# Earlier weight sums, paired snapshots and scaling moved to the output stage, in a linear-attention plus bilinear-FFN kernel

## The chip, the cores and the metric

The kernel runs on one core of a Trainium2 chip, as one program in one launch. The metric is device time in microseconds (us), from the start of the program to its end; lower is better. Engines are named as in the profile: PE is TensorE (PEld its weight loads), DVE is VectorE, ACT is ScalarE, POOL is GpSimd, and SP is the engine whose queue issues nearly all DMA transfers.

## The reference

The input is q, k and v of shape (4, 8, 768, 64) and one decay `lam` per head. A causal linear attention with decay is followed by a bilinear feed-forward network over 3072 tokens:

```python
for b in range(nb):                       # blocks of the sequence
    intra = np.einsum('bhic,bhjc->bhij', qb, kb) * Dmask[None]
    intra = np.einsum('bhij,bhjd->bhid', intra, vb)
    inter = np.einsum('bhid,bhde->bhie', qb * lam_pow[None], kv_state)
    out[:, :, sl] = intra + inter
    kv_state = lam_block * kv_state + np.einsum('bhsd,bhse->bhde', kb_dec, vb)
...
a = x @ w_a          # x: (3072, 512), the attention output; w_a, w_b: (512, 1536)
b = x @ w_b
return (a * b @ w_out).astype(np.float32)   # w_out: (1536, 512)
```

## The kernel before, in words

The tokens are cut into 24 units of 128 (6 units for each of the 4 batches). A unit's attention needs: its q, k and v loaded (`load_x`, three 256 KB transfers issued by SP); q and k scaled by powers of `lam` into one bf16 tile `qk` (`prep_k`: units 4 and 5 have k scaled on DVE and q on POOL, later units have both on POOL); that tile transposed (units 4 to 6 by PE, `piece_T`; from unit 7 on by a transposing DMA that SP issues, `dma_start_transpose`); v cast to bf16 (`prep_v`: POOL up to unit 6, DVE from unit 7); the scores on PE and their mask on DVE (`piece_S`, tiles `kq` and `m`); the state update (`piece_V`, tiles `kvd` and `st`); and the output (`pieces_O`), which ACT writes to the FFN's input `xT`.

The FFN takes the units in groups of 4, 1, 2, 4, 4, 4, 4 and 1 (groups 0 to 7). Groups 0, 1, 2 and 7 are computed directly: for each of 12 slices f of d_ff a product `a_ps`, a copy by ACT, a product `b_ps`, and the elementwise product `ab` by DVE, and after that the output products `op`. Groups 3 to 6 (`ffn_seven`) take pairs of slices (i = 0 to 5) with seven 128 by 256 products instead of eight. For this they need sums of the weights: `w_sums` makes the tile `tw` of pair i out of `wa_sb` and `wb_sb` with four elementwise sums of 128x512 bf16, and `sums` makes four sums `xs` of the group's `xT` on DVE. In `step(i, n)`, n names the product: the accumulating PSUM banks are copied by ACT at points in between (`snap`, tiles `s1`, `s2`, `s5`, `u2`), DVE adds `c12` and `c22`, and POOL adds `c11` out of the snapshots of products 1 and 2 and multiplies `c11` by `c12` into `ab`. The snapshot `s1` has two buffers and `s2` one.

The order of the work is written out by hand in `PLAN`: for each group a list of (slot, letter, unit). A group calls `hook(slot)` after each slice f (slots 0 to 11) and then in its output stage (from slot 12: for groups 3 to 6 two slots for each of the four output tiles, 12 to 19). P is `prep_k` and `prep_v` of a unit (PK and PV one of them), V, S, O, O2 and Q are pieces of the attention, C a weight cast, TW one call of `w_sums`, W the store of a kept output tile. Each engine runs its instructions strictly in the order in which they are issued here, and so does SP's queue.

Loads are issued ahead by `pump`, which is called after each weight cast and each `prep_v`. A unit may be loaded as long as it is less than `LOOKAHEAD` units beyond the last one whose q and k were scaled. A transfer also waits for a free buffer: q and k have three buffers each, v has four. Weights land in the pool `wst` (12 buffers of 4 KB per partition), which afterwards holds `tw`, `xs` and the kept outputs `o_kept` of the first seven units too; the outputs of later units go through three buffers `o_sb`.

Of the kernel before, what the change touches and what calls it, by code (L numbers as in the profile page):

```python
# [16 lines left out]
F32 = mybir.dt.float32  # L17
# [5 lines left out]
def _bc(ap, dims):  # L23
# [8 lines left out]
W_BUFS = 12  # L32
LOOKAHEAD = {9: 2, 10: 1}
# [10 lines left out]
PLAN = {  # L44
# [23 lines left out]


@with_exitstack  # L70
def kernel(
# [11 lines left out]
    nc = tc.nc  # L83
# [47 lines left out]

    def load_x(w, u):
        b, nb = divmod(u, NB)
        t = ld_pool.tile([128, H, D], F32, name=w + "f", tag=w + "f", bufs=4 if w == "v" else 3)
        nc.sync.dma_start(out=t, in_={"q": qr, "k": kr, "v": vr}[w][b, nb])  # L135
        raw[u, w] = t

# [55 lines left out]
    def pump():  # L193
        while pending:
            kind, c = pending[0]
            if kind in "abo":
                if len(staged) >= W_BUFS:
                    return
            elif c >= used["u"] + LOOKAHEAD.get(used["u"], 2 if used["u"] > 8 else 3):
                return  # L200
            pending.pop(0)
            if kind in "abo":
                load_w(kind, c)
            else:
                load_x(kind, c)
# [323 lines left out]
    def ffn_seven(g, u0, xT, hook):  # L529
# [20 lines left out]

        x11, x12, x22 = xT[:, 0:2, 0:256], xT[:, 2:4, 0:256], xT[:, 2:4, 256:512]

        def snap(name, ps, bufs):
            t = sn_pool.tile([128, 2, 256], F32, name=name, tag=name, bufs=bufs)
            nc.scalar.copy(t, ps)  # L555
            return t

        def step(i, n):
            d = live.setdefault(i, {})
            if n == 1:  # L560
                d["q"], d["qb"] = bank_of("m_q")
                product(i, d["q"], w_of(wa_sb, 0, i), x11, True)
                d["s1"] = snap("s1", d["q"], 2)
            elif n == 5:
                d["r"], d["rb"] = bank_of("m_r")
                product(i, d["r"], t_of(0, i), st[:, 0], True)
# [1 line left out]
            elif n == 2:  # L568
                p, pb = bank_of("m_p")
                product(i, p, w_of(wa_sb, 2, i), x12, True)  # L570
                s2 = snap("s2", p, 1)
                bank["held"].discard(pb)
                d["c11"] = a_pool.tile([128, 2, 256], BF16, name="c11", tag="a")
                nc.gpsimd.tensor_add(d["c11"], d["s1"], s2)  # L574
# [325 lines left out]
```

## Time and profile before

| | |
|---|---|
| median of 3 runs | 246.71 us (245.89 to 247.68) |
| the profiled execution | 246.64 us, of which the span from first to last instruction is 244.6 us |
| PE busy | 219.7 us, 90% |
| DVE, ACT, POOL busy | 145.1, 112.5 and 126.1 us |
| mean granted PE clock | 0.985 of full speed |

In answers on lines and waits, "out<-in" are the program's tile names, and what stands in brackets behind an instruction is the time that its engine sat idle before it and what ended this idle time. Times are from the start of the span.

### The profile page before, as it was taken

The page shows a single profiled execution, that of the slowest core. Times are in us where ns is not written, and L with a number is a line of the kernel's source. Part 1 is how long each engine was busy: PE and PEld are TensorE (multiplying, and loading weights), DVE is VectorE, ACT ScalarE, POOL GpSimd, SP SyncE. Part 2 cuts the span into 40 slices and gives each one's busy share as a digit, 9 for nine tenths or more (in the row PEclk, how much of TensorE's full clock was granted, in tenths as well). Part 3 has the DMA queues.
Part 4 walks back from the last instruction along what each step waited for, and adds up shares of the span by engine and source line. Part 5 has one row for each costly group of instructions (what it writes and reads, how often), then busy time and mean ns, then how long its engine had stood idle before and what let it go on. Part 6 is the DMA issues. An engine that isn't in the chain of part 4 may idle for free.

```text
span 244.6 us, 5389 instructions
## 1 busy us (share of the span) xinstructions
PE 219.7 (90%) x2108; PEld 151.2 (62%) x2127; DVE 145.1 (59%) x253; ACT 112.5 (46%) x220; POOL 126.1 (52%) x129
## 2 busy tenths in 40 slices
PE   7789999977996878499899979999979999999994
PEld 2565444446685646378555868546868547885493
DVE  1984748352679947647947746917757634664050
ACT  3685570153542136267124757235655236773151
POOL 6060001599995146968800899800999303874000
PEclk9999999997999999979999999999999999999999
DMA  4999999996819999990899398894590212000211
GB/s 146 302 288 350 374 386 288 231 214 132 133 36 179 184 190 221 227 216 4 170 163 387 113 197 137 170 176 171 24 193 14 50 71 86 0 3 6 102 68 44
DMA packets 97545, 39.41 MB, mean 161 GB/s; under 512 B 85488, under 2 KB 92016, under 8 KB 97520
## 3 DMA queue, kind: packets, MB, share of 16 engines
q1 hardware_dynamic: 97232, 39.00, 70.6%
q8 instruction: 16, 0.26, 0.5%
q10 hardware_dynamic: 288, 0.07, 0.1%
q14 instruction: 9, 0.07, 0.1%
HBM read 28.32 MB, written 6.29 MB: 141 GB/s over the span
## 4 chain that ended last, share of the span: by engine, by line
PE 56%; DMA 17%; POOL 8%; issue 6%; SPq 5%; DVE 5%; ACT 2%; POOLq 0%; DVEq 0%; ACTq 0%
PE op L642 18%; PE m_q L541 14%; PE m_r L541 7%; DMA qf<-in_q_dram 4%; PE a_ps L474 4%; PE b_ps L474 4%; DMA wst<-in_moe_w_a_dram 3%; PE m_p L541 3%; DMA wst<-in_moe_w_b_dram 3%; SPq L135 3%; POOL qk L281 3%; DMA kf<-in_k_dram 2%; PE o_ps L371 2%; DMA q<-in_q_dram 2%; DMA vf<-in_v_dram 2%
## 5 line engine op out<-in xcount | busy, mean ns | idle before, releaser
L642 PE MATMUL op<-wo_sb,ab 128*128 128x512 bf16 (+2 forms) x295 | 64.2, 362 | 1.5 <-issue 0.8
L574 POOL TENSOR_TENSOR c<-s,s 128x512 bf16<-128x512 f32 x24 | 30.5, 1272 | 44.9 <-ACT s L555 44.8
L541 PEld LDWEIGHTS <-tw 128*128 128x128 bf16 x384 | 37.8, 99 | 14.9 <-issue 7.2
L642 PEld LDWEIGHTS <-ab 128*128 128x128 bf16 x312 | 28.0, 98 | 27.8
L501 DVE TENSOR_TENSOR ab<-a_sb,b_ps 128x128 bf16<-128x128 bf16 (+2 forms) x48 | 19.3, 417 | 29.4 <-ACT a_sb L483 21.7
L281 POOL TENSOR_TENSOR qk<-qf,lp_q 128x512 bf16<-128x512 f32 x20 | 22.1, 1107 | 21.8 <-DMA qf<-in_q_dram 21.8
L354 DVE TENSOR_TENSOR m<-kq,lotri 128x512 bf16<-128x512 f32 x47 | 29.5, 684 | 5.2 <-PE kq L337 4.9
L541 PE MATMUL m_q<-xs,tw 128*128 128x256 bf16 x192 | 29.2, 275 | 2.7 <-ACT u L555 2.7
L583 POOL TENSOR_TENSOR ab<-c,c 128x512 bf16<-128x512 bf16 x24 | 28.2, 1174 | 4.4 <-DVE c L581 3.8
L474 PE MATMUL a_ps<-xT,wa_sb 128*128 128x128 bf16 (+2 forms) x198 | 28.3, 272 | 2.3 <-DVE ab L501 1.4
L474 PE MATMUL b_ps<-xT,wb_sb 128*128 128x128 bf16 (+2 forms) x192 | 28.1, 276 | 0.1
L590 DVE TENSOR_TENSOR ab<-c,m_q 128x512 bf16<-128x512 f32 x24 | 16.5, 687 | 19.3 <-PE m_q L541 19.3
L483 ACT CAST a_sb<-a_ps 128x128 bf16<-128x128 f32 (+2 forms) x48 | 17.4, 376 | 18.3 <-PE a_ps L474 15.4
L281 POOL TENSOR_TENSOR qk<-kf,lp_k 128x512 bf16<-128x512 f32 x18 | 19.1, 1063 | 11.3 <-DMA kf<-in_k_dram 8.7
L394 ACT CAST xT<-o_ps 128x512 bf16<-128x512 f32 (+1 forms) x24 | 12.2, 556 | 26.6 <-PE o_ps L371 26.5
L637 ACT COPY o_sb<-op 128x512 f32<-128x512 f32 (+2 forms) x19 | 10.3, 542 | 30.0 <-PE op L642 30.0
L474 PEld LDWEIGHTS <-wa_sb 128*128 128x128 bf16 x200 | 16.7, 101 | 9.3 <-issue 1.5
L581 DVE TENSOR_TENSOR c<-u,m_r 128x512 f32<-128x512 f32 x24 | 16.4, 682 | 8.7 <-ACT u L555 8.4
L541 PEld LDWEIGHTS <-wa_sb 128*128 128x128 bf16 x192 | 18.8, 99 | 3.0
L474 PEld LDWEIGHTS <-wb_sb 128*128 128x128 bf16 x192 | 16.1, 100 | 6.0 <-ACT wb_sb L174 0.2
L555 ACT COPY s<-m_r 128x512 f32<-128x512 f32 x24 | 14.1, 588 | 10.8 <-PE m_r L541 10.8
L555 ACT COPY s<-m_q 128x512 f32<-128x512 f32 x24 | 14.2, 590 | 10.6 <-PE m_q L541 10.2
(88 smaller groups left out, 307.5 us busy)
## 6 DMA issues: line engine op xcount, KB each, us to landing
vf<-in_v_dram SPq DMA_DIRECT2D x24, 256.0 KB, 4.9
qf<-in_q_dram SPq DMA_DIRECT2D x20, 256.0 KB, 4.2
kf<-in_k_dram SPq DMA_DIRECT2D x20, 256.0 KB, 4.6
out_dram<-o_sb SPq DMA_DIRECT2D x16, 256.0 KB, 2.1
wst<-in_moe_w_a_dram SPq DMA_DIRECT2D x6, 512.0 KB, 8.4
wst<-in_moe_w_b_dram SPq DMA_DIRECT2D x6, 512.0 KB, 8.8
wst<-in_moe_w_out_dram SPq DMA_DIRECT2D x6, 512.0 KB, 10.5
out_dram<-o_kept SPq DMA_DIRECT2D x7, 256.0 KB, 4.1
```

The costliest lines, as they stand in the source:

```text
L281: eng_of(eng).tensor_mul(dst.rearrange("p (c b) d -> p b c d", b=2), x[:].rearrange("p (b c) d -> p b c d", b=2), lp.rearrange("p (b c) o ...
L354: nc.vector.tensor_mul(m, kq[i], lotri_bc)
L474: nc.tensor.matmul(ps[:, lo:hi], lhsT=w_sb[:, s, f * 128:(f + 1) * 128], rhs=xT[:, s, lo:hi], start=(s == 0), stop=(s == KS - 1), skip_gro ...
L483: nc.scalar.copy(a_sb[:, :gt], ps[:, :gt])
L501: nc.vector.tensor_mul(ab[:, f, :gt], a_sb[:, :gt], ps[:, :gt])
L541: nc.tensor.matmul(ps[:, f, :], lhsT=w(k, f), rhs=x[:, k, :], start=(first and f == 0 and k == 0), stop=True, skip_group_check=True)
L555: nc.scalar.copy(t, ps)
L574: nc.gpsimd.tensor_add(d["c11"], d["s1"], s2)
L581: nc.vector.tensor_add(c12, d["u2"], d["r"])
L583: nc.gpsimd.tensor_mul(ab[:, 2 * i:2 * i + 2, 0:256], d["c11"], c12)
L590: nc.vector.tensor_mul(ab[:, 2 * i:2 * i + 2, 256:512], d["c22"], d["q"])
L642: nc.tensor.matmul(op[:, lo:hi], lhsT=ab[:, f, t * 128:(t + 1) * 128], rhs=wo_sb[:, f, lo:hi], start=(f == 0), stop=(f == FC - 1))
```

## The change

The edits, in the order of the diff:

- In groups 3, 4 and 5 the scaling and casting of units (P) leaves the product stage (slots 1, 3 and 9) for the output stage (slots 12, 14, 16, 18). Group 3 keeps two at slots 1 and 3 (units 13 and 14). The pieces Q, V and O2 of the output stage move one slot later.
- The six `w_sums` move: pairs 0 and 1 stay on POOL but are issued at slots 13 and 16 of group 0; pairs 2 and 3 go to DVE at slots 30 and 32 of group 0; pairs 4 and 5 stay on DVE, at slot 4 of group 1 and slot 15 of group 2.
- The pool `wst` has two more buffers (14), and v has three buffers instead of four.
- `pump` may load three units ahead instead of two from unit 17 on.
- The snapshots `s1` and `s2` become the halves of one tile `s12` out of the pool `wst`.

```diff
 for _g, _u in ((3, 11), (4, 15), (5, 19)):
     PLAN.setdefault(_g, []).extend(
-        [(1, "P", _u + 2), (3, "P", _u + 3), (9, "P", _u + 4), (11, "V", _u),
-         (12, "Q", (_u, _u + 1, _u + 2, _u + 3)), (14, "V", _u + 2),
-         (16, "O2", (_u + 2, _u + 3)), (18, "S", _u + 4)])
+        [(11, "V", _u), (12, "P", _u + 4), (13, "Q", (_u, _u + 1, _u + 2, _u + 3)),
+         (15, "V", _u + 2), (17, "O2", (_u + 2, _u + 3)), (18, "S", _u + 4)])
     if _u + 5 < 24:
-        PLAN[_g] += [(12, "P", _u + 5), (19, "S", _u + 5)]
+        PLAN[_g] += [(14, "P", _u + 5), (16, "P", _u + 6), (18, "P", _u + 7), (19, "S", _u + 5)]
+PLAN[3] += [(1, "P", 13), (3, "P", 14)]
 PLAN[3] += [(_s, "W", None) for _s in range(12, 19)]
-PLAN[0] += [(_s, "TW", (_f, "pool")) for _s, _f in ((31, 0), (34, 1))]
-PLAN[1] += [(_s, "TW", (_f, "pool")) for _s, _f in ((8, 2), (11, 3))]
-PLAN[2] += [(_s, "TW", (_f, "dve")) for _s, _f in ((3, 4), (5, 5))]
+PLAN[0] += [(_s, "TW", _f) for _s, _f in ((13, (0, "pool")), (16, (1, "pool")), (30, (2, "dve")),
+                                          (32, (3, "dve")))]
+PLAN[1] += [(4, "TW", (4, "dve"))]
+PLAN[2] += [(15, "TW", (5, "dve"))]
...
-    wst_pool = ctx.enter_context(tc.tile_pool(name="wst", bufs=W_BUFS))
+    wst_pool = ctx.enter_context(tc.tile_pool(name="wst", bufs=W_BUFS + 2))
...
-        t = ld_pool.tile([128, H, D], F32, name=w + "f", tag=w + "f", bufs=4 if w == "v" else 3)
+        t = ld_pool.tile([128, H, D], F32, name=w + "f", tag=w + "f", bufs=3)
...
-            elif c >= used["u"] + LOOKAHEAD.get(used["u"], 2 if used["u"] > 8 else 3):
+            elif c >= used["u"] + LOOKAHEAD.get(used["u"], 2 if 8 < used["u"] < 17 else 3):
...
-                d["s1"] = snap("s1", d["q"], 2)
+                d["s12"] = wst_pool.tile([128, 2, 2, 256], F32, name="s12", tag="wst")
+                snap("s1", d["q"], 0, d["s12"][:, 0])
...
-                s2 = snap("s2", p, 1)
+                snap("s2", p, 0, d["s12"][:, 1])
...
-                nc.gpsimd.tensor_add(d["c11"], d["s1"], s2)
+                nc.gpsimd.tensor_add(d["c11"], d["s12"][:, 0], d["s12"][:, 1])
```

How this moves instructions shows at three places (the number behind a tile's name tells one buffer's use from another). The first is POOL, from the last cast of weights in the front of the program to the work on unit 5. Before, q of unit 4 (`qk_690`) comes first, and the eight sums of pairs 0 and 1 (`tw_744`, `tw_780`) stand between it and q of unit 5 (`qk_788`):

```order
L178 CAST wa_sb_96<-wst_126 128x4x128
L281 TENSOR_TENSOR qk_690<-qf_495,lp_q_165 128x2x4x64
L300 CAST vb_740<-vf_534 128x512
L509 TENSOR_TENSOR tw_744<-wb_sb_97,wa_sb_96 128x512
L510 TENSOR_TENSOR tw_744<-wb_sb_97,tw_744 128x512
L511 TENSOR_TENSOR tw_744<-wb_sb_97 128x512
L512 TENSOR_TENSOR tw_744<-wa_sb_96,tw_744 128x512
L509 TENSOR_TENSOR tw_780<-wb_sb_97,wa_sb_96 128x512
L510 TENSOR_TENSOR tw_780<-wb_sb_97,tw_780 128x512
L511 TENSOR_TENSOR tw_780<-wb_sb_97 128x512
L512 TENSOR_TENSOR tw_780<-wa_sb_96,tw_780 128x512
L281 TENSOR_TENSOR qk_788<-qf_536,lp_q_165 128x2x4x64
```

In the change the same eight sums (`tw_668`, `tw_680`) stand ahead of q of unit 4 (`qk_700`) and of unit 5 (`qk_798`):

```order
L179 CAST wa_sb_96<-wst_126 128x4x128
L510 TENSOR_TENSOR tw_668<-wb_sb_97,wa_sb_96 128x512
L511 TENSOR_TENSOR tw_668<-wb_sb_97,tw_668 128x512
L512 TENSOR_TENSOR tw_668<-wb_sb_97 128x512
L513 TENSOR_TENSOR tw_668<-wa_sb_96,tw_668 128x512
L510 TENSOR_TENSOR tw_680<-wb_sb_97,wa_sb_96 128x512
L511 TENSOR_TENSOR tw_680<-wb_sb_97,tw_680 128x512
L512 TENSOR_TENSOR tw_680<-wb_sb_97 128x512
L513 TENSOR_TENSOR tw_680<-wa_sb_96,tw_680 128x512
L282 TENSOR_TENSOR qk_700<-qf_495,lp_q_165 128x2x4x64
L301 CAST vb_750<-vf_534 128x512
L282 TENSOR_TENSOR qk_798<-qf_536,lp_q_165 128x2x4x64
```

What moved: POOL does its eight sums before any unit's data, and q and v of units 4 and 5 then follow each other directly. The sums of pairs 2 and 3, which stood behind the v of unit 6, are gone from POOL.

The second place is DVE, from the second mask of unit 4 (`m1`) into the first products of group 1 (`ab`). Before, k of unit 5 (`qk_788`) follows the mask:

```order
L354 TENSOR_TENSOR m1_736<-kq1_725,lotri_149 128x512
L281 TENSOR_TENSOR qk_788<-kf_538,lp_k_166 128x2x4x64
L501 TENSOR_TENSOR ab_800<-a_sb_806,b_ps_808 128x128
L434 TENSOR_TENSOR st0_156<-kvd_312,bdiag_152 128x512
L501 TENSOR_TENSOR ab_800<-a_sb_824,b_ps_826 128x128
L501 TENSOR_TENSOR ab_800<-a_sb_837,b_ps_839 128x128
```

In the change:

```order
L355 TENSOR_TENSOR m1_746<-kq1_735,lotri_149 128x512
L510 TENSOR_TENSOR tw_752<-wb_sb_97,wa_sb_96 128x512
L511 TENSOR_TENSOR tw_752<-wb_sb_97,tw_752 128x512
L512 TENSOR_TENSOR tw_752<-wb_sb_97 128x512
L513 TENSOR_TENSOR tw_752<-wa_sb_96,tw_752 128x512
L510 TENSOR_TENSOR tw_763<-wb_sb_97,wa_sb_96 128x512
L511 TENSOR_TENSOR tw_763<-wb_sb_97,tw_763 128x512
L512 TENSOR_TENSOR tw_763<-wb_sb_97 128x512
L513 TENSOR_TENSOR tw_763<-wa_sb_96,tw_763 128x512
L282 TENSOR_TENSOR qk_798<-kf_538,lp_k_166 128x2x4x64
L502 TENSOR_TENSOR ab_810<-a_sb_816,b_ps_818 128x128
L435 TENSOR_TENSOR st0_156<-kvd_312,bdiag_152 128x512
```

What moved: the eight sums of pairs 2 and 3 (`tw_752`, `tw_763`) now stand ahead of k of unit 5 (`qk_798`), and with it ahead of everything that DVE does for group 1. A little further on, the four sums of pair 4 (`tw_895`) stand between the fifth and the sixth `ab` of group 1, where nothing stood before:

```order
L502 TENSOR_TENSOR ab_810<-a_sb_871,b_ps_873 128x128
L502 TENSOR_TENSOR ab_810<-a_sb_887,b_ps_889 128x128
L510 TENSOR_TENSOR tw_895<-wb_sb_97,wa_sb_96 128x512
L511 TENSOR_TENSOR tw_895<-wb_sb_97,tw_895 128x512
L512 TENSOR_TENSOR tw_895<-wb_sb_97 128x512
L513 TENSOR_TENSOR tw_895<-wa_sb_96,tw_895 128x512
```

The third place is SP's queue from the transposition of unit 15 on, with which the output stage of group 3 begins. Before, units 15 and 16 (`qkT_1751`, `qkT_1931`) are transposed, and the loads of units 17 and 18 issued, when the first store of the output stage comes:

```order
L309 DMA_TRANSPOSE qkT_1751<-qk_1748 128x8x128
L135 DMA qf_1755<-in_q_dram 128x8x64
L135 DMA kf_1757<-in_k_dram 128x8x64
L135 DMA vf_1759<-in_v_dram 128x8x64
L309 DMA_TRANSPOSE qkT_1931<-qk_1928 128x8x128
L135 DMA qf_1935<-in_q_dram 128x8x64
L135 DMA kf_1937<-in_k_dram 128x8x64
L135 DMA vf_1939<-in_v_dram 128x8x64
L626 DMA out_0_dram<-o_kept_751 128x512
L638 DMA out_0_dram<-o_sb_1948 128x512
L626 DMA out_0_dram<-o_kept_751 128x512
```

In the change the transposition of unit 16 (`qkT_1943`) stands behind three stores, and the loads of two units follow it:

```order
L310 DMA_TRANSPOSE qkT_1850<-qk_1847 128x8x128
L136 DMA qf_1854<-in_q_dram 128x8x64
L136 DMA kf_1856<-in_k_dram 128x8x64
L136 DMA vf_1858<-in_v_dram 128x8x64
L629 DMA out_0_dram<-o_kept_761 128x512
L641 DMA out_0_dram<-o_sb_1867 128x512
L629 DMA out_0_dram<-o_kept_761 128x512
L310 DMA_TRANSPOSE qkT_1943<-qk_1940 128x8x128
L136 DMA qf_1947<-in_q_dram 128x8x64
L136 DMA kf_1949<-in_k_dram 128x8x64
L136 DMA vf_1951<-in_v_dram 128x8x64
L136 DMA qf_1953<-in_q_dram 128x8x64
```

What moved: transpositions and loads of units 16 to 18 now alternate with the stores of the output stage, where before they stood ahead of them or in the next product stage.

More of the change, by code (lines that the diff above doesn't have):

```diff
@@ L551, in ffn_seven, with snap @@
         x11, x12, x22 = xT[:, 0:2, 0:256], xT[:, 2:4, 0:256], xT[:, 2:4, 256:512]
-        def snap(name, ps, bufs):
-            t = sn_pool.tile([128, 2, 256], F32, name=name, tag=name, bufs=bufs)
+        def snap(name, ps, bufs, t=None):
+            if t is None:
+                t = sn_pool.tile([128, 2, 256], F32, name=name, tag=name, bufs=bufs)
             nc.scalar.copy(t, ps)
```

## The prediction

> **What bounds the kernel now.** I read the engines' shares on the page first, then the list of who waited for whom on PE (in total, times, longest, us), then PE's granted clock in 40 slices of the span, and by stage (a row begins with the stretch, its length and PE's busy time; the clock is the number ahead of the DMA share).
>
> ```profile
> PE 219.7 (90%) x2108; PEld 151.2 (62%) x2127; DVE 145.1 (59%) x253; ACT 112.5 (46%) x220; POOL 126.1 (52%) x129
> PE tps L323 <- POOL qk L281: 3.1, 1, 3.1
> PE m_q L541 <- ACT u L555: 2.7, 4, 1.1
> PE m_r L541 <- DVE ab L590: 2.0, 1, 2.0
> PE m_q L541 <- DVE c L587: 1.4, 1, 1.4
> PE a_ps L474 <- DVE ab L501: 1.4, 1, 1.4
> PE kq L337 <- DVE ab L501: 1.4, 2, 0.8
> PE o_ps L371 <- DVE st L434: 1.2, 1, 1.2
> PE m_r L541 <- DVE xs L521: 1.1, 1, 1.1
> PE kq L337 <- DVE ab L590: 0.8, 2, 0.4
> PEclk9999999997999999979999999999999999999999
> 56.80:59.40 2.60, 2.60 (x25) 2.60 (x26) 0.29 (x1) 1.44 (x3) 2.60 (x4) 0.50 0.61 140
> 104.20:106.80 2.60, 2.60 (x14) 1.86 (x13) 0.85 (x2) 1.43 (x3) 2.15 (x2) 0.50 1.23 221
> 133.20:153.50 20.30, 18.88 (x174) 16.35 (x170) 13.09 (x21) 13.30 (x25) 17.78 (x16) 1.00 0.77 161
> 203.20:221.50 18.30, 18.30 (x167) 16.03 (x165) 10.11 (x17) 13.31 (x25) 13.12 (x11) 1.00 0.04 16
> ```
>
> PE is the bound: busy 219.7 of 244.6 us, and beside PE's own weight loads no engine reaches 60%. So time is won only where PE waits or runs at a lower clock. The nine waits add up to 15.1 us. Two slices fall below 9 tenths, behind two long waits: there PE ran 2.6 us at clock 0.50, which lost half of it, 1.3 us each; behind the other waits the clock stayed. The last two rows are the product stages of groups 4 and 6: group 4, with q and k scaled in between, leaves PE idle for 1.4 us; group 6, which has no such work, for nothing. All that can be won here is 15.1 + 2.6 = **17.7 us**. I go through these waits by place, each with what comes late next.
>
> **Unit 5's transposition (waits 3.1, half clock 1.3).**
>
> ```profile
> 25.79 1.05 ACT L174 CAST wb_sb<-wst 128x1024 bf16<-128x1024 f32 x1 [1.64 <-DMA wst<-in_moe_w_b_dram]
> 40.56 1.04 POOL L281 TENSOR_TENSOR qk<-qf,lp_q 128x512 bf16<-128x512 f32 x1 [21.79 <-DMA qf<-in_q_dram]
> 67.90 1.15 POOL L512 TENSOR_TENSOR tw<-wa_sb,tw 128x512 bf16<-128x512 bf16 x1
> 45.53 0.61 POOL L300 CAST vb<-vf 128x512 bf16<-128x512 f32 x1 [3.92 <-DMA vf<-in_v_dram]
> 56.79 1.03 PE L323 MATMUL tps<-ident,qk 128*128 128x128 bf16 x8 [3.12 <-POOL qk L281]
> 49.97 1.30 DVE L281 TENSOR_TENSOR qk<-kf,lp_k 128x512 bf16<-128x512 f32 x1
> 74.80 1.26 DVE L512 TENSOR_TENSOR tw<-wa_sb,tw 128x512 bf16<-128x512 bf16 x1
> 78.11 0.42 DVE L512 TENSOR_TENSOR tw<-wa_sb,tw 128x512 bf16<-128x512 bf16 x1
> 73.38 1.22 POOL L281 TENSOR_TENSOR qk<-kf,lp_k 128x512 bf16<-128x512 f32 x1
> ```
>
> PE reached this transposition at 53.7 and waited for q of unit 5, which stood behind eight sums on POOL. In the change these sums (1.15 us each, 9.2 in all) run in POOL's idle 21.8 us: they need the weights of pairs 0 and 1 and a free buffer, and the buffers that come free first held the weights whose cast ends at 26.8. So they end at about 27 + 9.2 = 36.2, ahead of 40.56: cost nothing. Were they to start after 31, they would push q of unit 4. q of unit 5 then goes as soon as its data are there: v of unit 4 landed at 45.5, and a load of 256 KB lands every 1.2 us while they queue (12.05 to 14.43 for two, in the part on the front), so q of unit 5 lands near 47, unit 6 near 51, unit 7 near 56.
>
> Next in line is k of unit 5 on DVE, now behind eight sums. The masks ahead of it end at 50.0 (DVE starts k at 49.97 today). A sum takes DVE 0.42 us with POOL at rest and 1.26 beside POOL's scaling, so eight take 3.4 to 10.1. POOL will scale unit 6 then, from about 51.5 to 53.6, so I take the first half near the low price and the rest in between: 4.5, then 0.7 for k, done at 55.2. PE waits 1.5 instead of 3.1; by the two ends, 0.4 or, with 1.3 for k, 7.7. Other waits of 1.4 left the clock alone, so that loss goes too. The Trainium skill (SBUF — State Buffer, section "SBUF: two separate sides") says that a VectorE operation with two SBUF inputs and a GpSimd operation that reads SBUF hold a shared port pair exclusively, one blocking the other for its whole length, which speaks against this edit; the trace agrees (0.42 against 1.26). By that rule, with POOL never pausing, the wait would be the 7.7 us end.
>
> The four sums of pair 4 come between the fifth and sixth `ab` of group 1.
>
> ```profile
> 53.06 0.39 PE L474 MATMUL a_ps<-xT,wa_sb 128*128 128x128 bf16 x4
> 53.29 0.39 PE L474 MATMUL b_ps<-xT,wb_sb 128*128 128x128 bf16 x4
> ```
>
> A slice takes PE two steps of 0.23 us, and on seven PSUM banks it can run three slices ahead, 1.3 us. Four sums last 1.7 to 5.0: PE waits 0.4 to 3.7. I take 0.7, as POOL is between units then.
>
> **Group 2 (1.4 + 1.4 + 1.2).** The first two waits are for `ab` behind the sums of pairs 4 and 5 on DVE, which leave this stage. The 1.2 is a state copy that DVE did late, behind the cast of unit 11's v, whose load is late for the reason told below for group 3. I leave half of the 1.4 on `kq`, 0.7, since two units' scores need four banks there whatever DVE does; bounds 0 and 1.4.
>
> **Group 3 (1.1 + 1.4 + 2.0, half clock 1.3).**
>
> ```profile
> 71.08 1.33 SPq L309 DMA_TRANSPOSE qkT<-qk  x1
> 81.77 0.57 SPq L135 DMA_DIRECT2D qf<-in_q_dram  x1
> 96.85 1.21 DVE L300 CAST vb<-vf 128x512 bf16<-128x512 f32 x1 [1.47 <-DMA vf<-in_v_dram]
> 101.54 1.05 DVE L300 CAST vb<-vf 128x512 bf16<-128x512 f32 x1 [2.29 <-DMA vf<-in_v_dram]
> 65.12 0.70 DVE L300 CAST vb<-vf 128x512 bf16<-128x512 f32 x1
> ```
>
> DVE's casts of v wait for loads, and the products behind them for DVE. The loads are late because unit 7 is scaled only after the last sum on POOL at 69.0, so SP transposes it at 71.1 and issues unit 11's loads at 81.8. Without these sums unit 7 is scaled when its data land, near 57. With one v buffer less, SP is held until v of unit 7 is cast (65.1 today, some 2 us earlier then). So SP's queue moves up by about 10 us and PE arrives only some 6 earlier (3.1 + 1.3 - 1.5 - 0.7 and 4.0 - 0.7): all waits of this stage go. The sums of pair 5 stand ahead of these casts, in DVE's idle time (1.5 us at 96.85): 1.7 to 5.0 us of work, I take 0.3 of delay, up to 3.5. The work of units 13 and 14 still stands among POOL's products, which end late for the output stage: 0.4.
>
> **Groups 4 and 5 (2.7 + 0.8).**
>
> ```profile
> 141.41 0.59 ACT L555 COPY s<-m_p 128x512 f32<-128x512 f32 x1 [0.67 <-POOL c L574]
> 135.57 1.27 POOL L574 TENSOR_TENSOR c<-s,s 128x512 bf16<-128x512 f32 x1 [13.88 <-ACT s L555]
> 132.95 0.40 PE L337 MATMUL kq<-qkT 64*128 64x128 bf16 x8
> 127.09 0.38 SPq L638 DMA_DIRECT2D out_dram<-o_sb  x1
> qkT<-qk SPq DMA_TRANSPOSE x17, 3.7
> vf<-in_v_dram SPq DMA_DIRECT2D x24, 256.0 KB, 4.9
> ```
>
> ACT's copy of `m_p` into its single buffer must wait until POOL has read the last one (0.67 at 141.41), and POOL lags by its scalings; `u` is copied behind it, and PE waits for `u`. With the scalings out of the stage and three or more buffers for `s12` both causes go; either alone would do. The wait on `kq` goes with Q one slot later.
>
> The moved work costs in the output stage: eight scalings, 8 x 1.05 = 8.4 us, in POOL's 13.9 us of idle time; two casts of v more on DVE (0.7 at 65.12, 1.2 at 96.85), counted as nothing because no wait of PE on DVE is left in these stages but the one on `kq`; loads and transpositions on SP between the stores. There the transposition of unit 16 must follow the first `o_sb` store (127.1 to 127.5) and a kept one: issued at 128.0, landed 3.7 later at 131.7, for scores at 132.95. `xs` comes one slot, 1.3 us, later; PE waits for it nowhere today but in group 3, so I count nothing (bounds in the last rival). v of unit 18 is issued 1.3 + 2 x 0.6 behind that, at 130.5, and lands 4.9 later, at 135.4; its cast stands ahead of unit 16's masks, whose scores are done at 133.4. Other PSUM banks let PE go on meanwhile; I take 0.6, between 0 and 2. If this cover goes, it is the second rival.
>
> **The front.** With three v buffers the fourth v waits for the first cast.
>
> ```profile
> 5.53 6.10 SPq L135 DMA_DIRECT2D vf<-in_v_dram  x4
> 12.05 0.61 POOL L300 CAST vb<-vf 128x512 bf16<-128x512 f32 x1 [7.38 <-DMA vf<-in_v_dram]
> 14.43 0.62 POOL L300 CAST vb<-vf 128x512 bf16<-128x512 f32 x1 [0.58 <-DMA vf<-in_v_dram]
> ```
>
> That cast ends at 12.7; evenly spaced, the last of the four issues began at 10.1. So SP, with all weights behind it, is up to 2.6 us later. But the third v lands only at 14.4, so the DMA engines stay busy meanwhile, which hides most: 0.5. The two buffers more in `wst`, and three units of loads from unit 17 on, cost nothing: they can only free transfers earlier.
>
> **Sum.** -17.7 + 1.5 + 0.7 + 0.7 + 0.3 + 0.4 + 0.6 + 0.5 = -13.0. The profiled execution took 246.6 us (span 244.6), 0.1 below the median of the runs: **233.6 us**.
>
> **Rivals.**
> - *Group 1 at POOL's pace.* The sums ahead of unit 5 take 10.1 and those of pair 4 5.0: 6.2 + 1.3 (clock) + 3.0 more: 244.1. For it: 1.26 in the trace; against: POOL has gaps while data land.
> - *The output stage of group 3.* SP's fuller queue brings unit 16's transposition and unit 18's v some 5 us late, and the clock falls: 233.6 + 6.3 = 239.9. For it: margins of 1.3 us; against: transfers there are issued in 0.6 us each.
> - *The loads do not come forward*, because SP waits for DVE's casts with a buffer less: group 3 keeps its 5.8: 239.4. The earlier sums then do nothing for the loads.
> - *Slower.* VectorE's SBUF work is paced by GpSimd all over: group 1 as above (+10.5), pair 5 (+3.2), and `xs` in three output stages, now beside scalings, four at 1.26 instead of 0.42, 3.4 late each, of which I take half as slack (3 x 1.7 = +5.1): 233.6 + 18.8 = 252.4. To pass 246.7 it needs 13.1 of these 18.8, a mean of about 1.0 us for a sum; against it, POOL should have finished its scalings when `xs` comes.
>
> **Chances.** Forecast (228 to 237) 0.62, group 1 0.09, output stage 0.13, loads 0.10, slower 0.06. The range takes in the second and third rivals: 228 to 241; below 228 lies nothing that the waits give. A measurement of this kernel tells 1% from no change: faster 0.89, within 0.05, slower 0.06.
>
> **What would show it.** Right: POOL's first eight sums start near 27; unit 5's transposition waits 1 to 2 us for DVE, not POOL; no DVE cast of v waits for DMA in group 3; product stages of groups 4 and 5 last 19 us; the clock stays at 1.00. Wrong: sums on DVE at 1.2 us; PE waiting at the start of group 4 for a mask or `qkT`; a later first weight cast.

## The result and the profile after

The changed kernel takes 237.31 us (median of four runs, 233.81 to 241.45) where the kernel before takes 246.30 on the same chip; the ratio is **0.952**, 95% interval 0.942 to 0.962. Two of the four runs (239.27, 241.45) had a mean TensorE clock of 0.978 against 0.993 and 1.000 in the others; this ratio and those below leave out runs over 1.5% above their kernel's best (here these two), while medians and ranges have all runs, and the profile comes from the first. The profiled span is 237.6, 7.0 below that of before.

First PE's share and the granted clock in 40 slices on the page, then the list of PE's waits (total, times, longest).

```profile
PE 221.4 (93%) x2127; PEld 151.8 (64%) x2127; DVE 154.8 (65%) x261; ACT 112.2 (47%) x220; POOL 120.6 (51%) x121
PEclk9997999999799999799999999999999999999999
PE m_q L542 <- DVE c L590: 3.6, 2, 2.8
PE tps L324 <- DVE qk L282: 3.6, 1, 3.6
PE a_ps L475 <- DVE wa_sb L177: 2.5, 1, 2.5
PE o_ps L372 <- DVE st L435: 0.5, 1, 0.5
PE op L645 <- DVE m L355: 0.3, 1, 0.3
```

Leaving out the program's two ends, nine rows of waits for other engines with 15.1 us have become five of 10.5; three single waits are long, all for DVE, and there are three slices at 7 tenths of the clock instead of two. By stage, with PE's idle time as the length less PE's busy time:

```profile
70.88:91.48 20.60, 20.13 (x241) 14.95 (x240) 15.65 (x30) 7.69 (x18) 6.31 (x6) 1.00 1.20 182
91.48:114.62 23.14, 20.31 (x182) 17.02 (x180) 17.79 (x27) 13.39 (x25) 17.89 (x15) 0.93 0.88 145
129.30:149.15 19.85, 19.09 (x178) 16.46 (x177) 13.67 (x22) 13.53 (x25) 15.45 (x13) 1.00 1.18 242
162.00:182.08 20.08, 20.08 (x183) 16.89 (x183) 15.06 (x25) 13.39 (x25) 14.00 (x12) 1.00 0.48 111
```

Group 2 (first row) has 0.5 us of idle time left, the products of group 4 (third row) 0.8, those of group 5 none. Group 3's products (second row) still have 2.8. Counted from the first product to the first `op`, the product stages of groups 4 and 5 last 19.4 and 18.4 us (before 20.2 each; the prediction's sign was 19). The stages, from the starts of PE's first instruction in each; the forecast column sorts the prediction's terms by stage:

| stretch | before | changed | difference | forecast |
|---|---|---|---|---|
| to the first `op` of group 0 | 40.02 | 42.81 | +2.8 | +0.5 |
| from there to group 2 | 27.41 | 28.07 | +0.7 | -2.2 |
| group 2 | 24.54 | 20.60 | -3.9 | -3.3 |
| products of group 3 | 25.44 | 23.14 | -2.3 | -5.1 |
| from there to the end | 127.2 | 123.0 | -4.2 | -2.9 |
| span | 244.6 | 237.6 | -7.0 | -13.0 |

The **front**. SP's issues of v, DVE's first weight cast (before, then in the change) and PE's first use of it:

```profile
5.57 7.47 SPq L136 DMA_DIRECT2D vf<-in_v_dram  x4
17.76 0.43 DVE L176 CAST wa_sb<-wst 128x384 bf16<-128x384 f32 x1 [0.71 <-DMA wst<-in_moe_w_a_dram]
19.77 0.42 DVE L177 CAST wa_sb<-wst 128x384 bf16<-128x384 f32 x1 [2.71 <-DMA wst<-in_moe_w_a_dram]
20.26 5.12 PE L475 MATMUL a_ps<-xT,wa_sb 128*128 128x256 bf16 x24 [2.48 <-DVE wa_sb L177]
```

SP ends its v issues 1.4 us later than before (13.04 against 11.63), and the cast starts 2.0 later.

**Unit 5's transposition.** POOL's first and last sum of pairs 0 and 1, four of the eight sums on DVE with k of unit 5 behind them, POOL's scalings beside them, and PE:

```profile
28.48 1.46 POOL L510 TENSOR_TENSOR tw<-wb_sb,wa_sb 128x512 bf16<-128x512 bf16 x1 [7.70 <-ACT wb_sb L175]
38.04 1.16 POOL L513 TENSOR_TENSOR tw<-wa_sb,tw 128x512 bf16<-128x512 bf16 x1
52.76 0.41 DVE L510 TENSOR_TENSOR tw<-wb_sb,wa_sb 128x512 bf16<-128x512 bf16 x1
53.21 1.31 DVE L511 TENSOR_TENSOR tw<-wb_sb,tw 128x512 bf16<-128x512 bf16 x1
56.82 0.42 DVE L511 TENSOR_TENSOR tw<-wb_sb,tw 128x512 bf16<-128x512 bf16 x1
57.50 1.26 DVE L513 TENSOR_TENSOR tw<-wa_sb,tw 128x512 bf16<-128x512 bf16 x1
58.69 1.52 DVE L282 TENSOR_TENSOR qk<-kf,lp_k 128x512 bf16<-128x512 f32 x1
53.20 1.04 POOL L282 TENSOR_TENSOR qk<-kf,lp_k 128x512 bf16<-128x512 f32 x1 [1.73 <-DMA kf<-in_k_dram]
57.21 1.27 POOL L282 TENSOR_TENSOR qk<-kf,lp_k 128x512 bf16<-128x512 f32 x1 [1.04 <-DMA kf<-in_k_dram]
58.45 1.22 POOL L282 TENSOR_TENSOR qk<-qf,lp_q 128x512 bf16<-128x512 f32 x1
60.27 0.40 PE L324 MATMUL tps<-ident,qk 128*128 128x128 bf16 x4 [3.58 <-DVE qk L282]
```

The eight sums on DVE last from 52.76 to 58.69, 5.9 us: those that meet no work of POOL take 0.42 (52.76, 56.82), those that run beside its scalings some 1.3 (53.21, 57.50), and k takes 1.5. The wait has changed its engine, POOL to DVE, and is no shorter.

**Group 3.** Pair 5's last two sums, the cast of v of unit 13, the `c` that PE needs, POOL beside the sums, and PE:

```profile
93.91 1.50 DVE L512 TENSOR_TENSOR tw<-wb_sb 128x512 bf16<-128x512 bf16 x1
95.33 1.26 DVE L513 TENSOR_TENSOR tw<-wa_sb,tw 128x512 bf16<-128x512 bf16 x1
96.51 1.26 DVE L301 CAST vb<-vf 128x512 bf16<-128x512 f32 x1
98.29 0.67 DVE L590 TENSOR_TENSOR c<-s,m_q 128x512 f32<-128x512 f32 x1
93.81 1.31 POOL L577 TENSOR_TENSOR c<-s 128x512 bf16<-128x512 f32 x1 [5.50 <-ACT s L557]
95.08 1.22 POOL L282 TENSOR_TENSOR qk<-kf,lp_k 128x512 bf16<-128x512 f32 x1
99.02 1.01 PE L542 MATMUL m_q<-xT,tw 128*128 128x256 bf16 x4 [2.83 <-DVE c L590]
```

No cast of v waits for a load any more in these rows; pair 5's first two sums took 0.41 and 0.43, the last two, beside POOL's work, three times as long, and they hold the cast and the `c` behind it.

### The profile page after: what moved, and what is told of

Read it like the earlier page. It is cut to its first block, busy times and chain, and to the rows that moved or that the text cites. A ratio compares the mean times of both kernels' runs of the same rounds, so it can differ in the third digit from the quotient of the medians.

```text
span 237.6 us, 5417 instructions
## 1 busy us (share of the span) xinstructions
PE 221.4 (93%) x2127; PEld 151.8 (64%) x2127; DVE 154.8 (65%) x261; ACT 112.2 (47%) x220; POOL 120.6 (51%) x121
## 4 chain that ended last, share of the span: by engine, by line
PE 61%; DMA 20%; SPq 8%; DVE 7%; POOL 1%; issue 1%; ACT 0%; POOLq 0%; DVEq 0%
PE op L645 19%; PE m_q L542 17%; PE m_r L542 8%; SPq L136 5%; DMA vf<-in_v_dram 5%; DMA kf<-in_k_dram 4%; PE m_p L542 4%; PE a_ps L475 4%; PE b_ps L475 4%; DMA wst<-in_moe_w_b_dram 4%; DMA wst<-in_moe_w_a_dram 4%; PE o_ps L372 3%; DMA q<-in_q_dram 2%; DVE vb L301 2%; SPq L158 2%; DMA qf<-in_q_dram 2%
## 5 line engine op out<-in xcount | busy, mean ns | idle before, releaser
L645 PE MATMUL op<-wo_sb,ab 128*128 128x512 bf16 (+2 forms) x312 | 67.4, 363 | 0.3 <-DVE m L355 0.3
L577 POOL TENSOR_TENSOR c<-s 128x512 bf16<-128x512 f32 x24 | 30.9, 1289 | 26.3 <-ACT s L557 26.3
L282 POOL TENSOR_TENSOR qk<-kf,lp_k 128x512 bf16<-128x512 f32 x18 | 19.4, 1078 | 32.3 <-DMA kf<-in_k_dram 28.6
L502 DVE TENSOR_TENSOR ab<-a_sb,b_ps 128x128 bf16<-128x128 bf16 (+2 forms) x48 | 19.3, 417 | 24.1 <-ACT a_sb L484 15.1
L475 PE MATMUL a_ps<-xT,wa_sb 128*128 128x128 bf16 (+2 forms) x200 | 29.8, 284 | 2.5 <-DVE wa_sb L177 2.5
L475 PE MATMUL b_ps<-xT,wb_sb 128*128 128x128 bf16 (+2 forms) x192 | 28.5, 279 | 0.0
L282 POOL TENSOR_TENSOR qk<-qf,lp_q 128x512 bf16<-128x512 f32 x20 | 22.8, 1140 | 3.3 <-DMA qf<-in_q_dram 3.3
L475 PEld LDWEIGHTS <-wa_sb 128*128 128x128 bf16 x200 | 17.5, 105 | 9.8 <-DVE wa_sb L177 2.6
L542 PEld LDWEIGHTS <-wa_sb 128*128 128x128 bf16 x192 | 18.8, 99 | 3.1
L542 PE MATMUL m_q<-xT,tw 128*128 128x256 bf16 x96 | 14.8, 278 | 3.6 <-DVE c L590 3.6
L590 DVE TENSOR_TENSOR c<-s,m_q 128x512 f32<-128x512 f32 x24 | 16.4, 684 | 1.0 <-PE m_q L542 0.6
```

Of the source, the lines that this page charges most:

```text
L282: eng_of(eng).tensor_mul(dst.rearrange("p (c b) d -> p b c d", b=2), x[:].rearrange("p (b c) d -> p b c d", b=2), lp.rearrange("p (b c) o ...
L475: nc.tensor.matmul(ps[:, lo:hi], lhsT=w_sb[:, s, f * 128:(f + 1) * 128], rhs=xT[:, s, lo:hi], start=(s == 0), stop=(s == KS - 1), skip_gro ...
L502: nc.vector.tensor_mul(ab[:, f, :gt], a_sb[:, :gt], ps[:, :gt])
L542: nc.tensor.matmul(ps[:, f, :], lhsT=w(k, f), rhs=x[:, k, :], start=(first and f == 0 and k == 0), stop=True, skip_group_check=True)
L577: nc.gpsimd.tensor_add(d["c11"], d["s12"][:, 0], d["s12"][:, 1])
L590: nc.vector.tensor_add(d["c22"], d["s5"], d["q"])
```

## The experiments

### One part alone, and all but one

```diff
 sums alone (e12), on the kernel before: the PLAN lines of "TW" as in the change's diff
 places alone (e11), on the kernel before: the PLAN lines of groups 3 to 5 as in the change's diff

 all but the places (e7), on the changed kernel
-        [(11, "V", _u), (12, "P", _u + 4), (13, "Q", ...
+        [(1, "P", _u + 2), (3, "P", _u + 3), (9, "P", _u + 4), (11, "V", _u), (13, "Q", ...
-        PLAN[_g] += [(14, "P", _u + 5), (16, "P", _u + 6), (18, "P", _u + 7), (19, "S", _u + 5)]
+        PLAN[_g] += [(12, "P", _u + 5), (19, "S", _u + 5)]
-PLAN[3] += [(1, "P", 13), (3, "P", 14)]

 all but the snapshots (e8), on the changed kernel
-    wst_pool = ...(name="wst", bufs=W_BUFS + 2))
+    wst_pool = ...(name="wst", bufs=W_BUFS))
-                snap("s1", d["q"], 0, d["s12"][:, 0])
+                d["s1"] = snap("s1", d["q"], 2)
-                snap("s2", p, 0, d["s12"][:, 1])
+                s2 = snap("s2", p, 1)
...
```

> The kernel before with nothing but the changed places of the weight sums (pairs 0 and 1 on GpSimd in group 0, 2 and 3 on VectorE at its end, 4 in group 1, 5 in group 2), four v buffers as before. Theory: group 2 takes 20.6 instead of 24.5 us and group 3's products 23 instead of 25.4, group 1 gains nothing (unit 5's transposition waits some 3 us for VectorE instead of GpSimd); 5.5 to 6.5 us in all, a span of 238 to 239. Rival: the gain of group 2 needs the later change of v buffers or places, and less than 3 is won.

> The kernel before with nothing but the changed places of the preparations (scalings of groups 3 to 5 in the output stage, Q, V and O2 a slot later). Theory: these places alone bring what groups 4 and 5 won: the way from group 3's output stage to group 4's 34.5 us and group 4's to group 5's 32.9 (before 36.1 and 35.1), nothing else moves, and the span is 244.6 - 3.8 = about 241 with the low clock as before. Rival: the scalings in the output stage are late because SP's loads stand between stores, and less than 1.5 is won.

> The changed kernel with the scalings of q and k of groups 3 to 5 back among the products (hook slots 1, 3, 9 and 12, as before); sums, buffers and snapshots as in the change. Theory: the shared snapshots with three or more buffers alone remove ACT's wait for GpSimd, so the products of groups 4 and 5 keep their time within 0.5 us each, and only the 0.8 us on kq come back: the way from group 3's output stage to group 4's lasts 34.5 to 35.3 us (before 36.1, changed 34.5), and group 4's to group 5's 33 to 33.8 (before 35.1, changed 32.9). Rival: GpSimd is late with or without the buffers, and both ways are back at 36 and 35 us, 3 us or more in all.

> The changed kernel with the two snapshots as separate tiles again (s1 two buffers, s2 one, 12 staging buffers), and the scalings in the output stage as in the change. Theory: without scalings GpSimd keeps up with the products and ACT never waits for it; the ways from output stage to output stage stay at 34.5 and 32.9 us within 0.4. Rival: one buffer of s2 is too few even so, and ACT waits about 0.7 us for GpSimd once or more per group, which PE feels by 1 to 2.7 us.

Measured: **sums alone** 238.03 us (ratio 0.969, 0.962 to 0.976; span 235.9 at full clock, better than the 238 to 239 expected; group 2 20.2 us); **places alone** 243.85 (0.9955, 0.992 to 0.999; span 241.4); **all but the places** (Q, V and O2 stay a slot later) 243.49 (0.985, 0.978 to 0.991); **all but the snapshots** (and the two staging buffers more) 235.94 (0.948, 0.942 to 0.954; span 232.6 at full clock). The sums are the larger part. The shared snapshots bring nothing that can be measured. The places bring 0.45% alone, less than the 3.8 us expected, and more beside the rest: without them the rest (0.985) is slower than the sums alone (0.969), so some of what else was changed costs time as long as the places are the old ones. The output stages follow each other like this (from the first `op` of a group to that of the next, us):

| | before | changed | places alone | all but snapshots | all but places |
|---|---|---|---|---|---|
| group 3 to 4 | 36.1 | 34.5 | 35.1 | 35.2 | 38.2 |
| group 4 to 5 | 35.1 | 32.9 | 33.9 | 32.8 | 34.3 |

With the places alone PE no longer waits for ACT's `u`, and with separate snapshots the time is that of the changed kernel. All but the places shortens the second way by 0.8, of which a wait of 0.4 on `kq` went with the later Q; neither its theory (33 to 33.8, and 34.5 to 35.3 for the first way) nor its rival came true. Its first way, 38.2, holds a wait of 3.6 us and a stretch of half clock behind it. The waits list has (line numbers in the experiments are up to two lower than in the changed kernel):

```profile
PE m_p L541 <- ACT o_sb L639: 3.6, 1, 3.6
PE op L644 <- POOL ab L585: 3.1, 2, 1.9
```

The 2.7 us that PE waited for ACT's `u` are gone, and 3.1 us for POOL's `ab` stand in the output stage instead: POOL is as late as it was, and PE now meets it later. The 3.6 is a copy of `o_sb` that waits 6.6 us for a store, which stood on SP behind two units' loads in a row. The sums alone, with the old places and the old lookahead, have one unit's loads ahead of these stores (114.82 to 117.07) and no such wait, so the third unit of lookahead is the likely cause; no run changes it alone. With the new places three stores go out ahead of the two units' loads, and the wait is gone.

### The front alone

```diff
-        t = ld_pool.tile([128, H, D], F32, name=w + "f", tag=w + "f", bufs=3)
+        t = ld_pool.tile([128, H, D], F32, name=w + "f", tag=w + "f", bufs=4 if w == "v" else 3)
-    wst_pool = ...(name="wst", bufs=W_BUFS + 2))
+    wst_pool = ...(name="wst", bufs=W_BUFS + 1))
```

> The changed kernel with four v load buffers again (as before), and 13 instead of 14 staging buffers so that they fit. Theory: the held fourth v load alone made the first weight cast 2.0 us late and set off the low clock behind it (1.5 us lost), so the first a_ps starts near 18.3 instead of 20.26 with a wait of 0.5 instead of 2.5, and a profiled span of 237.6 falls to 234 or 235.5. Rival: the first weights land late for another reason (their transfers share the memory with the other loads), the first a_ps still starts near 20.3, and the span stays within 0.5 us of 237.6.

Measured: 235.64 us (233.95 to 237.98; 0.956, 0.949 to 0.963); the first cast starts at 17.45 and PE's first `a_ps` at 17.93, as the theory had it, and the profiled span is 232.2. As a whole the kernel is not told apart from the changed one (0.952): what the front wins shows in its rows, not in the ratio. Over all profiles of this study the cast starts at 18.43 to 19.77 with three v buffers (six profiles, mean 18.96) and at 17.31 to 18.36 with four (eight, mean 17.69): the cost is 1.3 us on the mean, 2.0 in the profile shown. A second effect was not expected. The last sum ahead of k of unit 5, k itself, POOL's next scaling, the last sum of pair 4, and PE's wait:

```profile
52.20 0.41 DVE L513 TENSOR_TENSOR tw<-wa_sb,tw 128x512 bf16<-128x512 bf16 x1
52.54 0.68 DVE L282 TENSOR_TENSOR qk<-kf,lp_k 128x512 bf16<-128x512 f32 x1
52.93 1.19 POOL L282 TENSOR_TENSOR qk<-kf,lp_k 128x512 bf16<-128x512 f32 x1 [2.72 <-DMA kf<-in_k_dram]
57.52 1.26 DVE L513 TENSOR_TENSOR tw<-wa_sb,tw 128x512 bf16<-128x512 bf16 x1
59.03 0.96 PE L324 MATMUL tps<-ident,qk 128*128 128x128 bf16 x8 [2.60 <-DVE ab L502]
```

The same eight sums now run from 49.32 to 52.54, 3.2 us instead of 5.9, because all but the second (0.71) fall into a gap in which POOL waits for a load (the 2.72), and unit 5's wait is gone. Pair 4's sums, which took 0.42 each in the changed kernel (POOL waited for a load just then), now take up to 1.26, and PE waits 2.6 us for the `ab` behind them, at unit 6. What VectorE's sums cost is thus decided by where they fall against GpSimd's scalings, and a shift of the front is enough to move them.

### Where the sums stand

```diff
 e2, on the changed kernel (pairs 2 and 3 leave PLAN[0])
-PLAN[1] += [(4, "TW", (4, "dve"))]
+PLAN[1] += [(4, "TW", (4, "dve")), (8, "TW", (2, "dve")), (11, "TW", (3, "dve"))]
 e3, on the changed kernel (pair 5 leaves PLAN[2])
-PLAN[1] += [(4, "TW", (4, "dve"))]
+PLAN[1] += [(4, "TW", (4, "dve")), (8, "TW", (5, "dve"))]
 e4, on e1 (pairs 2, 3 and 5 leave their places)
-PLAN[1] += [(4, "TW", (4, "dve"))]
+PLAN[1] += [(2, "TW", (2, "dve")), (4, "TW", (4, "dve")), (8, "TW", (3, "dve")), (11, "TW", (5, "dve"))]
```

> The changed kernel with the sums of pairs 2 and 3 on VectorE moved from the output stage of group 0 into group 1's slices 8 and 11, so that k of unit 5 no longer stands behind them. Theory: the wait of 3.6 us at unit 5's transposition falls under 0.5, the half clock behind it (1.6 us lost) goes, and 4 to 5 us are won: about 233 against a profiled 237.6. Rival 1: with 12 sums in group 1 VectorE paces the gated products there, PE waits 3 us or more for ab, and less than 1.5 us is won. Rival 2: the time is given back in groups 2 and 3, whose loads do not come earlier.

> The changed kernel with the sums of pair 5 moved from slot 15 of group 2's hooks into group 1 behind slice 8. Theory: the wait of 2.8 us of PE for c in group 3 and the half clock behind it (1.4 us lost) were these sums alone, so 3.5 to 4.2 us are won: about 233.5 against a profiled 237.6. Rival: VectorE is late in group 3 because of its casts of v or of GpSimd's c11, and PE waits there for 1.5 us or more all the same.

> Four v buffers (13 staging buffers) and the sums of pairs 2 to 5 all in group 1 on VectorE, behind slices 2, 4, 8 and 11. Theory: the three long waits (2.5, 3.6, 2.8) were set by the v buffer and by where the sums stand, all three and their low clock go: 237.6 - 3.5 - 5 - 4 = about 225, clock 1.00. Rival: with 16 sums in group 1 VectorE becomes the bound there (3 us or more of waits for ab or masks), and 230 or more remains.

Measured: e2 238.55 us (234.36 to 241.42; too few comparable runs for a ratio), e3 234.84 (233.04 to 238.05; 0.952, 0.946 to 0.959), e4 234.93 (233.03 to 236.34; 0.955, 0.947 to 0.962). By the ratios neither e3 nor e4 is told apart from the changed kernel. Of e2's waits:

```profile
PE tps L323 <- DVE ab L501: 2.2, 1, 2.2
PE op L644 <- DVE ab L501: 0.7, 1, 0.7
```

Unit 5's wait is gone, and 2.9 us of waiting for `ab` have come in its place, near the 3 of the first rival. In e3 group 3's 2.8 fell to 1.2, and waits of 0.7 and 1.6 for `ab` appeared in group 1. In e4 all three long waits are gone, and group 1 waits 2.2, 1.4 and 0.9 for `ab`; a wait of 2.0 for a mask has come up at the start of group 4. Its spans of 231.3 to 234.6 miss the 225 of the theory by 6 to 10. In none of the three placements had VectorE room for more sums in group 1.

### The clock

The clock falls in stretches whose beginnings lie on a grid of 3.41 us. The changed kernel's three, each with the grid step ahead of it (the clock is the number ahead of the DMA share):

```profile
16.48:19.89 3.41, 1.30 (x34) 0.77 (x28) 0.70 (x2) 1.51 (x3) 0.09 (x1) 1.00 0.98 314
19.89:23.31 3.42, 3.05 (x15) 2.13 (x16) 2.13 (x4) 0.28 (x1) 0.89 (x2) 0.50 1.09 355
57.44:60.86 3.42, 0.59 (x11) 0.59 (x12) 3.42 (x5) 0.16 (x1) 2.23 (x2) 1.00 0.28 63
60.86:64.27 3.41, 3.41 (x38) 3.02 (x35) 2.86 (x11) 1.73 (x5) 0.73 (x1) 0.50 0.93 192
94.99:98.41 3.42, 1.19 (x11) 0.92 (x10) 3.42 (x5) 1.07 (x2) 2.50 (x3) 1.00 0.86 140
98.41:101.82 3.41, 2.80 (x14) 1.94 (x14) 2.92 (x4) 0.63 (x2) 3.31 (x3) 0.50 0.88 180
```

PE was idle for 2.1, 2.8 and 2.2 us of the step, and the next step ran at exactly half. In e1 the same wait of 2.83 us in group 3 lay across a border of the grid (1.14 and 1.69 us of idle time), and the clock stayed:

```profile
89.84:93.26 3.42, 2.28 (x20) 1.79 (x19) 3.42 (x4) 1.98 (x4) 3.42 (x3) 1.00 1.25 225
93.26:96.67 3.41, 1.72 (x16) 1.55 (x16) 3.41 (x6) 0.75 (x2) 2.39 (x3) 1.00 0.51 96
96.67:100.08 3.41, 3.41 (x34) 3.05 (x33) 2.42 (x5) 2.50 (x5) 3.41 (x4) 1.00 1.10 217
```

Leaving out the program's two ends, nine profiles of this study show 16 such falls. Fifteen follow a step with 1.86 us of idle time or more, one (in e7) a step with 1.4; of five other steps with 1.58 to 1.92 none was followed by one. The other five profiles (e2, e5, e6, e8, e12) have no fall and, on the grid that the first change of their clock gives, no step with more than 1.96; the 2.8 us that PE waits for `c` in group 3 of e2 and e8 lie across a border there too. So each of the 13 steps with 2.0 us or more was followed by a fall, and two of the five with 1.86 to 1.96. The Trainium skill (TensorE: Matmul & The Clock Gate, section "What's actually happening") has a free-running window of 3413 ns, with which the grid agrees; by its table the half rate comes after a whole idle window, while here some 2 us of idle time in a window were enough. In the next kernel the idle time is filled, and the waits are left:

```diff
+    def fill(n):
+        fps = ps_bank("fill", [128, 512], F32)
+        for _ in range(n):
+            nc.tensor.matmul(fps, lhsT=idle_sb[:, :128], rhs=idle_sb, ...)
 ahead of the first a_parts
+                    fill(9)
 in piece_T, ahead of tps
+        if u == 5:
+            fill(13)
 in ffn_seven, ahead of product 4
+                if g == 3 and i == 0:
+                    fill(10)
```

> The changed kernel with matmuls on zeros (their result is never read) put ahead of the three places where PE waits long: 9 ahead of the first a_ps (wait 2.5 us), 13 ahead of unit 5's transposition (3.6), 10 ahead of the first product that waits in group 3 (2.8), about 0.21 us each. The waits for data stay as they are. Theory: a stretch of half clock lasts 3.41 us, its beginnings lie on a grid of 3.41 us, and it comes when PE was idle for some 1.8 us or more of the 3.41 before; so with the idle time filled the clock is 1.00 in every run, and every run has a span of 232 to 233, the fastest of the changed kernel's. Rival: the low clock comes from the burst of work behind a wait or by chance; then runs of 0.978 and spans to 240 stay.

The page's clock row in this run:

```profile
PEclk9999999999999999999999999999999999999998
```

The clock was 0.997, 0.999, 0.993 and 0.998 in the four runs: so far the theory holds. The times were 235.22 to 239.61, not all at 234 (spans to 237.9 instead of 233). So the clock is not all of the spread between runs, and the theory's spans were not reached: span times mean clock, which takes its loss off, is 232.0 to 234.4 in the changed kernel's four runs and 232.7 to 236.2 in these. The added products have a price too: the 13 at unit 5 last 2.8 us whatever the wait is, and in the profile they held PE 0.6 us longer than k of unit 5 did (ready at 56.29, transposed at 56.93); where the wait is shorter, as in e8 (0.9), they would hold it longer. What else differs can't be seen in a run without a trace, and stays open.

### A better place for the sums

```diff
 e6, on e1
-... (16, (1, "pool")), (30, (2, "dve")), (32, (3, "dve")))]
+... (16, (1, "pool")), (24, (3, "pool")), (28, (2, "dve")))]
-PLAN[2] += [(15, "TW", (5, "dve"))]
+PLAN[2] += [(7, "TW", (5, "pool"))]
 e9, on e6: pairs 2 and 3 elsewhere
+PLAN[0].insert(PLAN[0].index((29, "S", 4)), (29, "TW", (2, "dve")))
+PLAN[1] += [(4, "TW", (4, "dve")), (13, "TW", (3, "dve"))]
 e10, on e9
-PLAN[3] += [(1, "P", 13), (3, "P", 14)]
+PLAN[3] += [(3, "P", 13), (6, "P", 14)]
```

> Four v buffers (13 staging buffers), and the sums where an engine is idle: pair 3 on GpSimd behind q of unit 4 in group 0, pair 2 on VectorE ahead of unit 4's masks (idle for 3.3 us there), pair 4 as in the change, pair 5 on GpSimd in group 2 (idle for 8 us there). Theory: it is VectorE's work around group 1 and the start of group 3 that PE waits for, so unit 5's wait of 3.6 us and group 3's of 2.8 us both go, with the front's 2.0 to 2.3: 232.1 at full clock becomes 224 to 226, and the clock stays at 1.00. Rival: the loads or GpSimd's scalings take the place of the sums as what is late (waits of 2 us or more for qk or vb), and 229 or more remains.

> As e6_place, but pair 2 on VectorE in slot 29, behind the last cast of wo and ahead of unit 4's masks, and pair 3 on VectorE at the end of group 1 (idle for 2.6 us there) instead of on GpSimd. Theory: the 2.4 us that PE waited in e6_place for a cast of wo came from two engines doing sums and casts at once (sums 1.26 to 1.6 us each there); with one engine at a time the wait goes, and a span of 230.4 at full clock becomes 228 to 229. Rival: pair 2 now delays unit 4's masks and k of unit 5, and the sums of pair 3 the casts of v: 230 or more.

> As e9_place2, and units 13 and 14 prepared at slots 3 and 6 of group 3 instead of 1 and 3. Theory: VectorE's casts of v 13 and 14 waited 0.9 and 2.1 us for their loads in e6_place and held the sums of products behind them, for which PE waited 2.0 us; later casts find their loads landed, and 1.5 to 2 us are won against e9_place2. Rival: SP's loads of units 15 to 17 hang on these preparations and come later, the output stage of group 3 waits for qk or vb: no gain or a loss of 1 to 2.

Measured: e6 233.72 us (232.30 to 235.72; ratio to before 0.948, 0.942 to 0.954), **e9 232.79** (232.02 to 233.87; 0.950, 0.945 to 0.956), e10 233.15 (232.19 to 234.49; 0.952, 0.944 to 0.959). In e6 the sums on both engines at once cost 0.8 to 1.6 each, PE waited 2.4 us for a cast of `wo` and, in group 3, 2.0 for an `ab` behind a cast of v whose load was late; the 224 to 226 expected was not reached. In e9 pair 2's sums cost 0.41 to 0.83, that wait is gone, and the list begins:

```profile
PE tps L324 <- DVE ab L502: 2.3, 1, 2.3
PE m_p L542 <- DVE m L355: 1.4, 1, 1.4
```

Its median is 4.5 us below that of the changed kernel and its runs lie within 1.9 us, not 7.6; its best run is 1.8 below that kernel's best. By the ratios (0.950 and 0.952, with overlapping intervals) it is not shown to be faster; what can be seen in these four runs is that it spreads less. The 228 that was expected is not reached: `ab` behind pair 4's sums (the 2.3) and a mask at the start of group 4 (the 1.4) are still waited for. e10 gained nothing: the 2.0 us of e6 that it was to win are not in e9's list any more, and its later preparations made PE wait 1.7 us for `qkT`, its rival.

## Why the prediction was right, and where its terms were wrong

The time forecast, 233.6, lies at the fast end of what was measured (233.8 at full clock, median 237.3). Its large claim held: the sums, taken from POOL's queue and from DVE in group 2, clear group 2 and part of group 3, and the places clear groups 4 and 5. At full clock the errors nearly cancel, which is luck in part. The kernel with separate snapshots has a profile at clock 1.00 and stands in here for the changed kernel, which has none; it has +0.4, -1.3, -3.5, -3.5 and -4.0 in the five stretches of the table, -12.0 in all (its start of group 2 is 66.50, of group 3 87.51, of the output stage 109.44). The profiled run of the changed kernel lost 5.0 us more: 2.4 up to the first `op` and 2.0 up to group 2, where two of its three stretches of half clock lie, and 1.2 in group 3's products with the third, less 0.6 in the rest.

- **Front, 0.5 of up to 2.6: mis-sized.** It delays the first cast by 1.3 us on the mean and by 2.0 in the profile, where half clock follows. That the DMA engines stay busy does not hide it in this profile: PE waits for one transfer, and that is issued late.
- **POOL's eight sums** start at 28.5 (forecast 27) and end at 39.2 instead of 36.2, at 1.15 to 1.6 each. q of unit 4 still waits for its load, to 42.1: nothing lost, as forecast.
- **Unit 5, wait 1.5: mis-sized in the profiled run, 3.6.** The step that failed is the price of the work on DVE ahead of the transposition: 4.5 for eight sums, which is 3.2 (e1) or 5.9 by POOL's work beside them, and 0.7 for k, which took 1.5 beside a scaling. The mechanism (k behind the sums on DVE, 0.42 or 1.26) is the one named, and the stage won nothing.
- **Pair 4, 0.7:** 0 in the profiled run, 2.6, 2.3 and 2.4 in e1, e9 and e10, whose fronts have four v buffers, and 0.9 in e6. Its bounds (0.4 to 3.7) held, the value did not.
- **Group 2:** gone, as forecast; also the 0.7 left on `kq` is gone, and 0.5 on a state copy stayed.
- **Group 3, "all waits go":** wrong. Loads do come earlier, though by 5 us (unit 11's at 76.6, before 81.8), not 10; the casts wait for none. But pair 5, priced 0.3, costs 2.8 and the clock: in e3, without these sums, the wait is 1.2. The measured 2.8 lies under the upper bound of 3.5; DVE's "idle time" was a wait for loads, and the loads had come.
- **Groups 4 and 5:** -4.2 against -2.9. v of unit 18 is late for 0.8 (forecast 0.6). "Either alone would do" was half wrong: the places do, the buffers move most of the wait. That three units of loads "cost nothing" held with the new places only: with the old ones they are the likely cause of the 3.6 above.
- **The clock stays at 1.00:** wrong in three of four runs. Its sum left no wait above 1.5 us, so it had no term for the clock; three waits of 2.5 to 3.6 came, and only the rivals had priced that. The two stretches before were 3.41 us long, not 2.6, and cost some 1.4 and 1.7 us instead of 1.3 each.
- **The rivals:** the first (group 1 at POOL's pace) came true in part: 2.1 us more of wait and the half clock, of its 10.5; the loads came forward; VectorE was not paced by POOL all over (`xs` 0.41 to 0.43, but for two of sixteen with 0.88 and 1.15).

## What to carry to other kernels

Before work is moved to an engine's idle time, ask what runs on the other engine at that moment, and price both cases; where the two differ threefold, as 0.42 and 1.3 us do here, the timing of an earlier stage can decide which you get. A buffer taken from the first loads can delay the first transfer behind it by all the time that its issue waits. A wait that is left is dearer than its length when some 2 us of it fall into one step of the clock: three waits of 2.5 to 3.6 us cost some 5 us more in the profiled run (clock 0.978 over 237.6 us), and that is part of why the same program spreads by 7.6 us.

## What the runs showed of the hardware

The clock is granted in steps of 3.41 us on a grid that does not start with the program; about 2 us of idle time in one step halves the next, so the same wait costs up to 1.7 us more (half of 3.41) or nothing by its place on the grid. In e4 the half clock lasted three steps, though PE was idle for only 1.2, 0.6 and 0.3 us of them:

```profile
59.06:62.47 3.41, 2.26 (x22) 2.26 (x22) 2.69 (x8) 1.18 (x2) 2.22 (x2) 0.50 1.22 218
62.47:65.89 3.42, 2.82 (x29) 2.27 (x27) 3.38 (x6) 0.80 (x3) 2.42 (x2) 0.50 1.21 191
65.89:69.30 3.41, 3.13 (x18) 1.01 (x19) 3.38 (x9) 0.00 (x0) 0.93 (x1) 0.50 1.33 221
```

What ends a stretch was not settled: in e11 (the places alone) it lasted two steps, the first with 0.95 us of idle time, but after one with 0.6 in the changed kernel the clock was back.

A sum of 128x512 bf16 takes VectorE 0.42 us where GpSimd does nothing and 1.26 to 1.5 beside its work, and GpSimd's scalings of 128x512 then take 1.2 to 1.3 us themselves instead of 1.04.
